# SyncE issues attention's loads and stores in the order of the program's steps

## The chip, the cores and the metric

The kernel runs on one core of one Trainium2 chip. The metric is the device time of one execution in microseconds (us). A core has five engines with an instruction queue each: TensorE (PE, matmuls), VectorE (DVE), ScalarE (ACT), GpSimd (POOL) and SyncE (SP). SP computes nothing here: it starts DMAs and reads a few numbers into its registers. Every queue runs in its own order, and an instruction that waits for a semaphore holds everything behind it in the same queue.

## The reference

Attention with a feature map comes first, then a mixture of experts. `phi` projects 64 values of a head to 128, subtracts the largest magnitude, and takes the exponentials of both signs.

```python
def phi(x):
    proj = np.einsum('bhsd,df->bhsf', x, w_phi)
    proj = proj - np.max(np.abs(proj), axis=-1, keepdims=True)
    return np.concatenate([np.exp(proj), np.exp(-proj)], axis=-1)
q_p, k_p = (phi(q), phi(k))
kv = np.einsum('bhsf,bhsd->bhfd', k_p, v)
z = np.sum(k_p, axis=2)
num = np.einsum('bhsf,bhfd->bhsd', q_p, kv)
den = np.einsum('bhsf,bhf->bhs', q_p, z)[..., None] + 1e-06
attn = num / den                      # 8 batches, 8 heads, 576 tokens, 64
...
x = attn.transpose(0, 2, 1, 3).reshape(4608, 512)
do_compute = x @ w_skip > 0           # the other tokens pass through
logits = xc @ w_gate                  # 8 experts, the largest is taken
h = np.maximum(xc[mask] @ w1[e], 0.0) # 512 -> 1024
y[mask] = gate_w[mask, None] * (h @ w2[e])
out[do_compute] = xc + y
```

## The kernel before

Matmuls run in fp32, or in two parts: a number is split into `hi` (rounded) and `lo` (the rest), and products of the parts are added.

**Units and items.** Attention works in units: four heads of one batch, of k or of q. There are 16 k units and 16 q units. A unit has five items: item 0 is the tail of 64 tokens, items 1 to 4 are four groups of the rest. Item s of the k stream is item s % 5 of k unit s // 5, and the same for q.

**Steps.** One loop (L724) goes through steps t. A stage with a lag works at step t on item t - lag of the k stream and on item t - 6 - lag of the q stream (`CFG["off"]` is 6). The order of the stages within a step is E, P, A, Z, U, T:

- T, lag 0 (`f_t`, L712): VectorE transposes a piece of the unit's `raw` tile (L289, L291; items 0, 1 and 3 only), ACT makes `hi` (L292), POOL or VectorE makes `lo` (L294). At item 0 of unit u it also issues the load of unit u + 1 of its stream (`st_load`, L256, four DMAs). So k unit u + 1 is loaded at step 5u, and q unit u + 1 at step 5u + 6. Four `raw` tiles exist, two for each stream in effect.
- P, lag 1 (`st_proj`): TensorE projects (L306 to L308), VectorE takes the maximum and subtracts it (L312, L321). Three PSUM banks.
- E, lag 3: exponentials; for k, POOL adds them up (`z`), for q, TensorE transposes first (L366).
- U, lag 4: k items are multiplied with `v` (L388, tails L395); q items with the k unit's sums (L486, L465), then `norm` on VectorE (L437 to L449) writes `xm`, `lgm`.
- Z and A, lags 5 and 6: sums over tokens and the augmented k sums.

Then, each step, `st_loadv` loads v of the k unit whose item 0 is one step old (L265, four DMAs, two buffers) and `st_loadvt` its tails at three steps (L274, four DMAs, two tiles).

**Stores.** What has to come some steps later stands in a list `later`, which is worked off at the head of a step (L730). When q item 4 of a batch's first unit is done, half of its rows go to `xrows` two steps later (`store_half`, L503 and for every second batch L505). When its second unit is done, `post(b)` computes the gate: a chain of some 14 small VectorE and ACT instructions (L538 to L561). Two steps later the other half goes out together with the gate (`store_rows`, L564, L566). Four steps later comes the rank among tokens (`rank`), five later `index`, seven later the copy of the rows to `out` (`rest`, L630 in four DMAs, L635 in four for every second batch). Two buffers of `xm` exist. After batch 5, `pick` chooses two experts and gathers their first tokens early.

**Order.** The program is traced in the order above. A scheduler then orders each engine's instructions by when it expects them to be ready, and by their place in the program where several are. Two things bind it: dependencies between tiles, and a manual schedule, inside which the named engines keep the program's order. Before the change PE has such a guard, from step 8 to step 78 (L725 to L728). SP has none.

**After attention.** The experts take their tokens in slots; weights come in 96 chunks of 512 KB through four `raw` buffers (L184, L187), are split by ACT (L188) and POOL or VectorE (L189), and multiplied (L881 to L913). Before the first chunk SP reads the chosen expert's number into a register (L1056).

Of the kernel before, what the change touches and what calls it, by code (L numbers as in the profile page):

```python
# [18 lines left out]
P = 128  # L19
# [5 lines left out]
def kernel(  # L25
# [25 lines left out]
    NAUG = D + E + 2  # L51
    NA1 = NAUG - 1
    # a row of xrows: the token, its gate, its number
    XW = DM + 2
    EB = B - 3
    NTE = 9 * (EB // 2) + 9
    # slots: full ones, ones of up to 192 tokens, ones of up to 128
    NSD = (NTOK + E * 63) // SLOT
# [22 lines left out]
    nc.scalar.activation(out=warm, in_=warm, func=AF.Exp)  # L81
    # w_phi in the rows of either head of a pair, and which rows are whose
    wsrc = const.tile([P, NF], F32, name="wsrc")
# [22 lines left out]
    iota_p = const.tile([P, P], F32, name="iota_p")  # L106
    # the tails of a quad's v, each pair in its own rows, zeros in the other's
    vts = [const.tile([P, 2, 2, D], F32, name="vt%d" % j) for j in range(2)]
# [14 lines left out]
    pad0 = const.tile([P, 2, 2], I32, name="pad0")  # L123
    # of every slot: the rows to gather and the rows to scatter to
    ft = const.tile([P, NSL, 4], I32, name="ft")
# [84 lines left out]
    def places(g, pad, v):  # L210
        # v is 0 in an empty place, else 1 + the row to gather; what to add so that no row is scattered from an empty one
        nc.vector.tensor_scalar(out=g, in0=v, scalar1=-1.0, scalar2=0.0, op0=ALU.add, op1=ALU.max)
        nc.vector.tensor_scalar(out=pad, in0=v, scalar1=0.0, scalar2=BIG, op0=ALU.is_equal, op1=ALU.mult)

    early = []
    # ------------------------------------------------------------------ attention
    with ExitStack() as actx:
# [4 lines left out]

        # a head is 32 runs of 18 tokens; partition (half of d, head of the pair, run)
        kv_in = {
# [4 lines left out]
        outv = out.rearrange("(b p j) m -> b p j m", p=32, j=18)  # L229
        # rows of xrows: two batches after each other, then the tails of both  # L230
        xr = xrows.rearrange("(b x) m -> b x m", x=2 * S)
# [201 lines left out]
        def norm(o, xdst, ldst, shape):  # L433
            # o: [P, 4, NAUG]
            den = small.tile([P, 4], F32, tag="den", name="den")
            rec = small.tile([P, 4], F32, tag="rec", name="rec")
            nc.vector.tensor_scalar(  # L437
                out=den.rearrange("p (t o) -> p t o", o=1), in0=o[:, :, NA1:NAUG],
                scalar1=1e-6, scalar2=None, op0=ALU.add,
            )  # L440
            nc.vector.reciprocal(out=rec, in_=den)
            rv = rec.rearrange("p (t o) -> p t o", o=1)
            a, c = shape

            def sh(x):
                return x.rearrange("p (a c) d -> p a c d", a=a)

            nc.vector.tensor_tensor(out=xdst, in0=sh(o[:, :, 0:D]), in1=sh(rv.broadcast_to([P, 4, D])), op=ALU.mult)
            nc.vector.tensor_tensor(  # L449
                out=ldst, in0=sh(o[:, :, D:NA1]), in1=sh(rv.broadcast_to([P, 4, NA1 - D])), op=ALU.mult)  # L450

        def st_use_q(u, i):
# [5 lines left out]
            if i == 0:  # L458
                # the tails of two batches side by side
                for h in range(4):  # L460
                    pr, hd = h // 2, h % 2
                    for half in range(2):
                        for par in range(2):
                            g = u.g - NQ * (1 - par)
                            nc.tensor.matmul(  # L465
                                ov[par * 64:par * 64 + 64, h, :],
                                et_of[g][:, half, hd * P + pr * 64:hd * P + pr * 64 + 64], kva_of[g][:, half, h, :],
                                start=(half == 0), stop=(half == 1),
                            )
                if u.hq == 0:  # L470
                    xt_of[u.b // 2] = (
                        xp.tile([P, 1, XW], F32, tag="xt", name="xt"),
                        xp.tile([P, 1, H, E + 1], F32, tag="lgt", name="lgt"),
                    )
                xt, lgt = xt_of[u.b // 2]
                norm(ov, xt[:, :, u.hq * 4 * D:(u.hq + 1) * 4 * D].rearrange("p a (h d) -> p a h d", d=D),
                     lgt[:, :, u.hq * 4:(u.hq + 1) * 4, :], (1, 4))
                return
# [34 lines left out]
        def post(b):  # L513
# [40 lines left out]
            )  # L554
            # the gate goes with the token's row
            nc.vector.tensor_reduce(out=ss[:, 0:nt], in_=ex[:, 0:nt], axis=AX.X, op=ALU.add)
# [20 lines left out]
            def rank():  # L577
                # rank of each computed token among those of its expert
                r = bank("O")[:, 0:nt * E]
# [66 lines left out]
        def pick(j):  # L646
            # the expert with the most tokens so far: its first tokens make a slot of their own, done early;
            # the ranks of its later tokens start anew
            cn = bank("O")[:, 0:E]
# [72 lines left out]

        man = None
        for t in range(n + OFF + LA):  # L724
            if CFG["man"] and t == CFG["man"][0]:  # L725
# [27 lines left out]
            if t == 1:  # L753
                setup()

    # ------------------------------------------------------------------ experts
    pools = {}
# [31 lines left out]
    def hidden_c(hv):  # L789
        # 192 tokens: the last 64 with both their parts next to each other  # L790
        hh = mo.tile([P, 2, SLOT], F32R, tag="hh", name="hh", bufs=5)
        hlo = mo.tile([P, 2, SLOT], F32R, tag="hlo", name="hlo", bufs=5)
        n = P + 64
        nc.scalar.activation(out=hh[:, :, 0:n], in_=hv[:, :, 0:n], func=AF.Relu)
        for o, a, b in ((hlo[:, :, 0:P], 0, P), (hh[:, :, n:SLOT], P, n)):
            (nc.gpsimd if (CFG["cp"] >> (a == P)) & 1 else nc.vector).scalar_tensor_tensor(  # L796
                out=o, in0=hv[:, :, a:b], scalar=0.0, in1=hh[:, :, a:b].bitcast(F32), op0=ALU.max, op1=ALU.subtract)
        return hh.rearrange("p f t -> p (f t)"), hlo.rearrange("p f t -> p (f t)")

    def half1(ws, xs):  # L800
        # a slot of 128 tokens: the tokens' columns stay, the weights stream
        _, xh, xl, _, _ = xs
# [38 lines left out]
    def store_c(y, xs):  # L841
        xg, to = xs[0], xs[3]
        # the sums of the high and of the low parts of 64 tokens lie in either half of y
        g, x, r = xg[1][:, DM:DM + 1], xg[1][:, 0:DM], slice(0, 64)
# [10 lines left out]
    def mm1(ws, xs, hooks=()):  # L855
# [3 lines left out]
        for c, (wh, wl) in enumerate(ws):  # L859
            if n < SLOT:  # L860
                # fewer than 256 columns take as long as 256: the products with both parts of x side by side
                hsum = mo.tile([P, 2, n], F32, tag="hsum", name="hsum")
# [65 lines left out]

    # the slots of the tokens that are left: per expert full ones of 256, a rest of up to 192 or of up to 128 in
    # one of its own kind  # L930
    eid = const.tile([1, NSL], I32, name="eid")
# [4 lines left out]
    def tables():  # L936
# [23 lines left out]
        nc.vector.tensor_tensor(out=exc, in0=inc, in1=nn, op=ALU.subtract)  # L960
        # a token's column: its rank, in groups of 128, plus cf[0] where it is below cf[1], else plus cf[2]
        nc.vector.tensor_scalar(out=cf[:, 0], in0=exc[:, 0], scalar1=2.0, scalar2=1.0, op0=ALU.mult, op1=ALU.add)
# [6 lines left out]
        nc.vector.tensor_tensor(out=cf[:, 2], in0=cf[:, 2], in1=cf[:, 1], op=ALU.subtract)  # L969
        # the experts of the slots, and how many there are  # L970
        le = const.tile([1, NSL, E], F32, name="le")
# [6 lines left out]
        nc.vector.tensor_scalar(out=eid[:, 0:NSL], in0=ef, scalar1=float(E - 1), scalar2=None, op0=ALU.min)  # L978
        # the column of each token
        rk = const.tile([P, NT], F32, name="rk")  # L980
# [44 lines left out]
        places(ft[:, NS2:NSL, 0:1], ft[:, NS2:NSL, 2:3], ix[:, 2 * NS2:NCOL].rearrange("p (t s) -> p t s", s=1))  # L1025
        # the slots that the sequence below leaves
        ov = const.tile([1, 8], F32, name="ov")
# [6 lines left out]
        for c, to, left in ((0, 0, "DC"), (1, 3, "CS")):  # L1034
# [9 lines left out]
            out=ovf[:, 0:NSL], in0=lv[:, 1], scalar1=float(num["D"] - 1), scalar2=float(NSL - 1), op0=ALU.add, op1=ALU.min)  # L1044
    # the slots in their order; a half one goes along with a full one
    phases = []
# [48 lines left out]

    # whatever the slots above don't hold
    nx = nc.values_load(ovf[0:1, NSL:NSL + 1], min_val=0, max_val=NSL)  # L1097
# [37 lines left out]
```

## Time and profile before

| | us |
|---|---|
| median of 3 runs | 684.47 |
| lowest and highest run | 684.28, 689.55 |
| span of the profiled execution | 681.4 |
| first expert matmul (L881) begins | 389.78 |

The page gives busy time by engine, a strip of 40 slices with busy tenths, and groups of instructions. An answer of the trace in order of time has start, duration, engine, line and what the instruction writes and reads; in square brackets stands how long the engine was idle before it and what ended that. `SPq` is SP's queue, and the duration of one of its DMAs is the time for which SP was occupied by starting it, not the transfer. A view of waits has the waiting instruction, what it waited for, then the total, the number of times and the longest.

This is the strip of the page, and the largest waits of SP's queue in the whole span:

```profile
PE   4897999979998889999899991999999989979994
DVE  6868888887978978978998799679988876677830
DMA  9898664857675667655316387269788877774500
```

```profile
SPq L184 <- POOL w L189: 53.7, 15, 14.8
SPq L187 <- POOL w L189: 48.6, 20, 6.2
SPq L256 <- DVE m L312: 47.0, 18, 5.7
...
SPq L503 <- DVE lgm L449: 15.1, 2, 9.3
SPq L630 <- DVE lgm L449: 14.0, 3, 6.0
```

One slice is 17 us. Attention fills the first 22 or so, the experts the rest. The raw loads (L256) wait for VectorE, which frees their buffers; the name of the releaser is that of the instruction that ended last before the wait was over.

### The profile page before, as it was taken

To read this page: it belongs to the slowest core of one execution; us is meant where nothing else is said; L and a number is where in the kernel's file an instruction comes from. 1 tells how busy PE (TensorE), PEld (TensorE's weight loads), DVE (VectorE), ACT (ScalarE), POOL (GpSimd) and SP (SyncE) were. 2 spreads that over 40 slices of the span, in tenths; PEclk is the share of its full clock that TensorE was granted. 3 is DMA by queue.
4 is the path that set the end of the run, shared out by engine and by line. 5 is a ranking of instruction groups with operands and counts; after the bars stand their busy time and mean duration, and the time that the engine had idled before them with its cause. 6 is when DMAs were issued, how large, how long until landed. Compare 5 with 4: busy or idle time off the path is not lost. (4 is left out here: it accounts for less than half of the span.)

```text
span 681.4 us, 16258 instructions
## 1 busy us (share of the span) xinstructions
PE 600.5 (88%) x6045; PEld 514.2 (75%) x6045; DVE 539.6 (79%) x1216; ACT 373.7 (55%) x747; POOL 440.7 (65%) x383
## 2 busy tenths in 40 slices
PE   4897999979998889999899991999999989979994
PEld 3585888768877778877788881888878879868893
DVE  6868888887978978978998799679988876677830
ACT  4566665647565475656564533147757556555510
POOL 6886777777777596868774458276575485374411
PEclk9898999999999999999999996899989999999998
DMA  9898664857675667655316387269788877774500
GB/s 130 127 145 157 112 168 91 160 108 133 144 144 90 146 117 133 142 103 114 105 33 195 114 222 232 72 203 296 249 262 268 268 238 267 251 238 139 192 17 27
DMA packets 221684, 108.17 MB, mean 159 GB/s; under 512 B 160293, under 2 KB 202405, under 8 KB 221604
## 3 DMA queue, kind: packets, MB, share of 16 engines
q1 hardware_dynamic: 218272, 97.60, 58.8%
q0 software_dynamic: 3200, 9.45, 4.0%
q8 instruction: 49, 0.80, 0.5%
q14 instruction: 31, 0.25, 0.1%
q10 hardware_dynamic: 132, 0.07, 0.0%
HBM read 83.86 MB, written 24.02 MB: 158 GB/s over the span
## 5 line engine op out<-in xcount | busy, mean ns | idle before, releaser
L189 POOL TENSOR_TENSOR w<-wraw_c,w 128x1024 fp32r<-128x1024 f32 x45 | 109.9, 2454 | 70.6 <-ACT w L188 64.3
L188 ACT ACTIVATE w<-wraw_c 128x1024 fp32r<-128x1024 f32 x96 | 101.0, 1057 | 56.9 <-DMA wraw_c<-in_moe_w_dram 44.9
L353 POOL TENSOR_TENSOR z<-ek 128x512 f32<-128x512 f32 x64 | 81.7, 1277 | 54.9 <-ACT ek L345 45.1
L312 DVE TENSOR_REDUCE m<-ps_P 128x4 f32<-128x512 f32 (+1 forms) x160 | 96.4, 620 | 3.7 <-PE ps_P L308 3.6
L321 DVE TENSOR_TENSOR u<-ps_P,m 128x512 f32<-128x512 f32 (+1 forms) x160 | 95.9, 621 | 0.4
L306 PE MATMUL ps_P<-wph,hi 128*128 128x256 f32 x256 | 80.8, 316 | 16.6 <-ACT hi L292 8.5
L486 PEld LDWEIGHTS ps_O<-kva,eq 128*64 128x64 f32 x2048 | 75.2, 137 | 18.0 <-ACT eqt L373 7.3
L189 DVE TENSOR_TENSOR w<-wraw_c,w 128x1024 fp32r<-128x1024 f32 x51 | 75.4, 1481 | 14.6 <-ACT w L188 14.5
L486 PE MATMUL ps_O<-kva,eq 128*64 128x74 f32 x2048 | 78.4, 229 | 5.0 <-ACT eqt L373 3.2
L294 POOL TENSOR_TENSOR lo<-xT,hi 128x512 fp32r<-128x512 f32 x61 | 78.1, 1280 | 5.0 <-ACT hi L292 4.8
L308 PE MATMUL ps_P<-wph,lo 128*128 128x256 f32 x256 | 73.4, 287 | 0.0
L307 PE MATMUL ps_P<-wpl,hi 128*128 128x256 f32 x256 | 73.2, 286 | 0.0
L388 PE MATMUL ps_K<-ek,v 128*64 128x256 f32 x512 | 71.3, 396 | 1.5 <-DMA v<-in_v_dram 1.5
L372 ACT ACTIVATE eq<-ps_U 128x512 f32<-128x512 f32 x64 | 37.9, 593 | 57.2 <-PE ps_U L366 49.2
L306 PEld LDWEIGHTS ps_P<-wph,hi 128*128 128x128 f32 x256 | 49.4, 193 | 20.4 <-ACT hi L292 9.0
L908 PE MATMUL ps_O<-w,hh 128*128 128x512 f32 x160 | 62.4, 400 | 1.4 <-DVE hh L796 1.3
L836 POOL DMA_INDIRECT out_dram<-o,si x17 | 22.2, 1305 | 54.1 <-DVE o L834 44.4
L913 PE MATMUL ps_O<-w,hlo 128*128 128x512 f32 x120 | 49.0, 410 | 5.1 <-DVE hlo L796 5.1
L307 PEld LDWEIGHTS ps_P<-wpl,hi 128*128 128x128 f32 x256 | 49.7, 194 | 0.0
L308 PEld LDWEIGHTS ps_P<-wph,lo 128*128 128x128 f32 x256 | 49.6, 194 | 0.2 <-DVE lo L294 0.2
L366 PE MATMUL ps_U<-ident,u 128*128 128x128 f32 x288 | 48.4, 286 | 0.6 <-DVE u L321 0.6
L289 DVE STREAM_TRANSPOSE xTt<-raw 128x128 f32<-128x128 f32 x32 | 9.9, 309 | 48.8 <-DMA raw<-in_k_dram 26.8
(233 smaller groups left out, 1570.9 us busy)
## 6 DMA issues: line engine op xcount, KB each, us to landing
wraw_c<-in_moe_w_dram SPq DMA_DIRECT2D x96, 512.0 KB, 4.6
raw<-in_k_dram SPq DMA_DIRECT2D x64, 144.0 KB, 4.0
raw<-in_q_dram SPq DMA_DIRECT2D x64, 144.0 KB, 4.1
v<-in_v_dram SPq DMA_DIRECT2D x64, 128.0 KB, 3.7
out_dram<-xm SPq DMA_DIRECT2D x32, 256.0 KB, 4.4
xrows<-xm SPq DMA_DIRECT2D x8, 516.0 KB, 4.2
xrows<-xm SPq DMA_DIRECT2D x8, 512.0 KB, 4.7
vt<-in_v_dram SPq DMA_DIRECT2D x64, 16.0 KB, 2.6
```

The lines of the kernel that those rows point to most:

```text
L188: nc.scalar.activation(out=hi, in_=raw, func=AF.Copy)
L189: (eng or nc.vector).tensor_tensor(out=lo, in0=raw, in1=hi.bitcast(F32), op=ALU.subtract)
L294: (nc.vector if CFG["ini"][nlo[0] - 1:nlo[0]] == "v" else nc.gpsimd).tensor_tensor(out=lo, in0=xT, in1=hi.bitcast(F32), op=ALU.subtract)
L306: nc.tensor.matmul(o, hi[:, c], wph, start=True, stop=False)
L307: nc.tensor.matmul(o, hi[:, c], wpl, start=False, stop=False)
L308: nc.tensor.matmul(o, lo[:, c], wph, start=False, stop=True)
L312: nc.vector.tensor_reduce(out=m[:, 0:nt], in_=pv, axis=AX.X, op=ALU.max, apply_absolute_value=True)
L321: nc.vector.tensor_tensor(out=uu[:, 0:nt, :], in0=pv, in1=m[:, 0:nt].rearrange("p (t o) -> p t o", o=1).broadcast_to([P, nt, NF]), op=ALU. ...
L353: zeng.tensor_tensor(out=z, in0=e[:, 0:2, :], in1=e[:, 2:4, :], op=ALU.add)
L388: nc.tensor.matmul(o[hd * 64:hd * 64 + 64, :], u.v[:, 2 * pr + hd, g * D:(g + 1) * D], u.e[i][:, 2 * j + hd, :], start=(g == 0), stop=False,)
L486: nc.tensor.matmul(ov[s * 64:s * 64 + 64, 2 * j + hd, :], e[:, half, j, hd, s * 64:s * 64 + 64], kva[:, half, 2 * pr + hd, :], start=(half ...
L908: nc.tensor.matmul(y[sub], hh[:, t], wh[:, fi, :], start=first, stop=False)
```

## The change

The loop over the steps is put into a second manual schedule, for SP, from the first step to the last. Inside it SP issues its DMAs in the program's order: at each step first what `later` holds, then the raw loads, then v, then the tails. The first k unit's load (called at L698, before the loop), the last batch's copy to `out` and all that belongs to the experts stay outside. Nothing is fenced at the guard's end by the code. Some comment lines go, so the lines after shift little.

```diff
         man = None
+
+        sman = actx.enter_context(ExitStack())
+        sman.enter_context(tc.manual_schedule(engines={mybir.EngineType.SP}))
         for t in range(n + OFF + LA):
             if CFG["man"] and t == CFG["man"][0]:
                 man = ExitStack()
                 man.enter_context(tc.manual_schedule(engines={mybir.EngineType.PE}))
             if CFG["man"] and t == CFG["man"][1]:
                 man.close()
...
             if t == 1:
                 setup()
+        sman.close()
```

## Prediction

> **What bounds the kernel now.** I read the page for the whole, busy time by stretch for the stage that the change touches, then the waits of PE and DVE in it, and last SP's queue and DVE in order of time. Times are us from the span's start; in a timeline the columns are start, duration, engine, line, what it does.
>
> ```profile
> span 681.4 us, 16258 instructions
> PE 600.5 (88%) x6045; PEld 514.2 (75%) x6045; DVE 539.6 (79%) x1216; ACT 373.7 (55%) x747; POOL 440.7 (65%) x383
> ```
> ```profile
> core 0: us, PE busy (x) PEld busy (x) DVE busy (x) ACT busy (x) POOL busy (x), PEclk, DMA share, GB/s
> 60.00:345.00 285.00, 263.35 (x3470) 221.72 (x3469) 240.46 (x680) 175.12 (x415) 216.06 (x206) 1.00 0.61 125
> ```
> ```profile
> DVE xTt L289 <- DMA raw<-in_k_dram: 20.6, 11, 2.4
> DVE xTt L289 <- DMA raw<-in_q_dram: 16.5, 10, 3.4
> ...
> PE ps_O L619 <- POOL rhs L608: 7.5, 6, 1.6
> PE ps_P L306 <- DVE u L321: 5.9, 9, 1.5
> PE ps_O L486 <- ACT eqt L373: 3.2, 4, 1.1
> PE ps_O L486 <- DVE lgm L449: 1.4, 2, 0.8
> PE ps_O L406 <- DVE acc L625: 1.3, 3, 0.7
> PE ps_P L306 <- DVE km L549: 1.1, 1, 1.1
> PE ps_O L580 <- DVE lgm L449: 1.1, 1, 1.1
> ```
>
> The second fence is the steady part of attention: PE is busy 263.35 of 285 at full clock (92%), in an order fixed by its own guard. The third holds the waits of DVE and PE there. DVE is busy 240.46 and idle 44.5, of which 20.6 + 16.5 = 37.1 is spent in front of a transpose whose raw tile has not landed; 7.4 is left. PE waits for DVE in all 5.9 + 1.4 + 1.3 + 1.1 + 1.1 = 10.8, and for no DMA in this stretch. So PE sets the pace, DVE is close behind, and a late raw load reaches PE only by way of DVE.
>
> **How far SP's order differs from the program's.**
>
> ```profile
> 93.54 3.31 SPq L256 DMA_DIRECT2D raw<-in_k_dram  x4
> ...
> 103.87 2.19 SPq L256 DMA_DIRECT2D raw<-in_q_dram  x3
> 106.15 0.82 SPq L503 DMA_DIRECT2D xrows<-xm  x1
> 107.02 0.64 SPq L256 DMA_DIRECT2D raw<-in_q_dram  x1
> ...
> 120.37 2.08 SPq L265 DMA_DIRECT2D v<-in_v_dram  x4
> 122.55 0.84 SPq L274 DMA_DIRECT2D vt<-in_v_dram  x2
> ...
> 129.77 3.51 SPq L630 DMA_DIRECT2D out_dram<-xm  x4
> ...
> 139.34 0.57 SPq L564 DMA_DIRECT2D xrows<-xm  x1
> 140.01 0.57 SPq L566 DMA_DIRECT2D xrows<-xt  x1
> ```
> ```profile
> 90.09 0.57 SPq L564 DMA_DIRECT2D xrows<-xm  x1
> ...
> 323.61 0.57 SPq L564 DMA_DIRECT2D xrows<-xm  x1
> ```
> ```profile
> 112.19 0.31 DVE L289 STREAM_TRANSPOSE xTt<-raw 128x128 f32<-128x128 f32 x1 [2.92 <-DMA raw<-in_q_dram]
> ...
> 128.29 0.18 DVE L449 TENSOR_TENSOR lgm<-ps_O,rec 128x36 f32<-128x36 f32 x1
> ...
> 139.20 0.12 DVE L561 RECIPROCAL xt<-gt 128x1 f32<-128x1 f32 x1
> ```
>
> Batch b's gate store L564 belongs to the step at which post(b) has run plus 2: post(1) runs at step 29 (item 19 of the q stream, plus off 6, plus lag 4), its store at the head of step 31. Loads of q unit u stand at step 5(u-1)+6, so q unit 6 (the seventh q load, 103.87) stands at step 31 too, behind the store. In the trace it goes out 35 ahead of it. The next four v loads of step 31 go at 120.37, 19 ahead of the store. After the change both stand behind L564, and L564 waits for the gate chain on DVE, whose last piece ends at 139.32. From one even batch's store to another odd one's, 90.09 to 323.61, lie five batches of ten steps: 233.52 / 50 = 4.67 per step.
>
> **The change part by part.** It adds no arithmetic and removes none; 318 DMAs of attention on SP (252 of raw, v and vt loads, 2 of gate weights, 24 stores to xrows, 40 to out) keep their size and number, and those after the first 50 us change their place.
>
> *Stores moved up.* L503, L505, L564, L566, L630 and L635 no longer follow later steps' loads. Nobody in attention reads xrows or out before the early gather, so an earlier store gains nothing. Cost 0; that holds as long as the tile of two batches on (two buffers) is not waiting for it.
>
> *Loads moved down, behind the gate store.* Queued behind the waiting L564 are q unit 6 (4 DMAs), v of k unit 6 (4), its tails (4), k unit 8 (4), then the next stores and q unit 7. With L564 at 139.34 as now, SP issues L564 and L566 (1.24 to 140.6), four q loads (2.19 + 0.64, to 143.4) and four v (2.08, to 145.5).
>
> ```profile
> raw<-in_q_dram SPq DMA_DIRECT2D x64, 144.0 KB, 4.1
> v<-in_v_dram SPq DMA_DIRECT2D x64, 128.0 KB, 3.7
> ```
>
> With these medians from issue to landing the q tile lands at 147.5 and v at 149.2. PE did step 29 up to DVE's norm at 128.47. It first needs v of k unit 6 at step 35 (item 31 plus lag 4): 128.47 + 6 x 4.67 = 156.5, a cover of 7.3. It needs q unit 6 at step 37: 165.8, a cover of 18.3, of which a transpose and the split into hi and lo take an estimated 4. K unit 8 follows after vt (four at 0.42) and four issues of 0.83: issued by 150.5, wanted at step 41, 184.5. So the loads that are 35 later still arrive in time for PE, once per batch, with v the closest. Cost on PE's path 0; what hides it is PE's own work of steps 30 to 34, and if the gate chain ended 8 later, each further us would be paid seven times.
>
> *DVE's waits for raw tiles.* The scheduler places a transpose where it expects the tile, and DVE then stands. Now that is 37.1 over some 10.5 pairs of units, 3.5 a pair. What it becomes behind long runs of DMAs is not in the steady part; the nearest rows are the start, where SP's order is already that of the steps, with 16 DMAs between one k unit and the next:
>
> ```profile
> 31.85 3.26 SPq L256 DMA_DIRECT2D raw<-in_k_dram  x4
> ...
> 43.75 4.24 SPq L256 DMA_DIRECT2D raw<-in_k_dram  x4
> ```
> ```profile
> 38.66 0.31 DVE L289 STREAM_TRANSPOSE xTt<-raw 128x128 f32<-128x128 f32 x1 [1.56 <-DMA raw<-in_k_dram]
> ...
> 43.06 0.31 DVE L289 STREAM_TRANSPOSE xTt<-raw 128x128 f32<-128x128 f32 x1 [1.06 <-DMA raw<-in_q_dram]
> ...
> 51.23 0.31 DVE L289 STREAM_TRANSPOSE xTt<-raw 128x128 f32<-128x128 f32 x1 [3.97 <-DMA raw<-in_k_dram]
> ...
> 55.21 0.31 DVE L289 STREAM_TRANSPOSE xTt<-raw 128x128 f32<-128x128 f32 x1 [0.61 <-DMA raw<-in_q_dram]
> ```
>
> Those two pairs stand 1.56 + 1.06 = 2.6 and 3.97 + 0.61 = 4.6. The lower end for the steady part is 0 a pair (no tile late any more), which would give DVE 37.1 back and PE at most its 10.8 of waits. Between two gate stores, ten steps, stand 16 raw, 8 v and 8 vt loads and on average 9 stores, 41 DMAs. The upper end takes the worse pair for every 16 of them: 4.6 x 41 / 16 = 11.8 per batch in place of 7.0, or 28 over six batches. I take 4.6 a pair, because the runs get longer, not shorter: 1.1 x 10.5 = 11.6 more on DVE, of which PE feels the share that it feels now, 10.8 / 37.1 = 0.29: +3.4.
>
> SP's issue time carries this term: in the rows above four raw loads take 2.8 to 4.2 of SP and land 4.1 after. The Trainium skill says of this (DMA: Bandwidth & Descriptors, section "Issuing engines are not separate DMA queues") that the time in which a sequencer starts a DMA is usually small beside the DMA; by that the run's length would not matter and the sum would be 0. These rows contradict it here, so I keep +3.4.
>
> *The end of attention.*
>
> ```profile
> 362.68 3.23 SPq L630 DMA_DIRECT2D out_dram<-xm  x4
> 366.12 0.92 SPq L184 DMA_DIRECT2D wraw_c<-in_moe_w_dram  x1
> 368.01 0.53 SPq L564 DMA_DIRECT2D xrows<-xm  x1
> ```
> ```profile
> 384.38 1.05 ACT L188 ACTIVATE w<-wraw_c 128x1024 fp32r<-128x1024 f32 x1
> ```
>
> The weights' first loads lie outside the guard and can go before or after these stores. They are out from 366.12 and ACT splits the first chunk only at 384.38, so ten us either way are covered: 0. If they had to wait for the last gate store they would start some 31 later; nothing in the code ties them to it.
>
> Sum: 0 + 0 + 3.4 + 0. The profiled span is 681.4, the median of the runs 684.47, 3.07 more, which I keep: 684.47 + 3.4 = 687.9.
>
> **The rivals.** *DVE becomes the bound (slower).* At the upper end DVE stands 28 longer. It has 7.4 of other idle time to give; what is beyond that is paid in full: +20.6, 705. For it: busy 240.46 plus 37.1 of standing is 97% of the stretch. Against: two pairs at the start show no growth from one to the next run beyond 2.
>
> *Late v starves PE (slower).* Decides once L564 goes out more than 7.3 later against PE than now. At 12 later each of seven batches pays 5: +35, 719. Against: the gate chain's instructions are small and earlier in the program than what delays them. The Trainium skill's advice to issue a DMA early and wait late (DMA: Bandwidth & Descriptors, "Rules for kernel authors") points to this rival; no row of this case shows PE short of v in the stretch.
>
> *DVE stops standing (faster).* Loads no longer follow directly on the transpose that frees their buffer, and the tile could be there before DVE gets to it. That takes the 37.1 away and with it up to 10.8 of PE: 673.7. It decides when the load leads DVE's place for it by more than the 4.1 of landing. Against: DVE's order is made for the earliest place, so it moves with the load.
>
> **How the numbers follow.** Likeliest, the covers hold and DVE stands a little longer: 0.53, 687.9, own range 681 to 692. DVE bound: 0.22, 692 to 706. Late v: 0.08. No standing: 0.17, 673 to 681. A range of 676 to 706 leaves out late v and about half of the last. One per cent is 6.8, about what a measurement of this kernel tells from no change: below 677.6 lie 0.13 (most of no standing); above 691.3 lie 0.22 + 0.08 and 0.03 of the likeliest, 0.33; between them 0.54.
>
> **What would show it.** Right: in SP's queue the q load stands behind L564 in its step, waits of SP sit at L564 and L503, PE in the steady stretch still waits for no v, and DVE's waits for raw lie between 37 and 49. Wrong: PE waiting for v or vt at L388 or L395; DVE's waits for raw over 60 or under 20; weights that start only after the last L564.

## The result, and the profile after

| us | before | after |
|---|---|---|
| median of the runs | 684.38 (682.85 to 689.55, 4 runs) | 736.99 (733.11 to 738.56, 4 runs) |
| ratio to before | | 1.073, 95% interval 1.068 to 1.079 |
| span of the profiled execution | 681.4 | 731.3 |
| first expert matmul begins (L881, after L885) | 389.8 | 439.6 |

The change costs 52.6 us. The forecast, 687.9 in a range of 676 to 706, was wrong by 49. Lines behind L754 lie four higher after the change.

All of it is lost ahead of the experts: they take 270.4 us from their first to their last such matmul before (389.8 to 660.2), and 270.6 after (439.6 to 710.2).

The strip of the page after, 18.3 us a slice:

```profile
PE   3889889759879859879859999289997989998994
...
PEclk9999999989999979999989999689999999998998
DMA  8876186095287087186075277627888788685500
GB/s 129 128 106 117 41 157 135 2 184 125 41 168 136 1 170 155 39 155 134 7 170 109 89 209 211 204 92 218 264 256 276 256 246 285 230 262 176 192 16 25
```

Up to us 340 the DMA row before never fell under 3. Now there are slices with 2, 1 and 7 GB/s (the 8th, 14th and 20th): for nearly 20 us at a time next to nothing is loaded. In the slice after each of them PE falls to 5 tenths and PEclk to 8 or 7.

To compare the same work I take the stretch from the first to the last matmul L619 over the ranks. First before, then after: the row of that line (instructions, then shortest, median and longest in ns, then first and last start), and busy time in that stretch, in the columns of the prediction's second fence:

```profile
L619 PE MATMUL ps_O<-rhs,OP x54: 175/176/178, 99.1 to 331.9; 128*128 128x32 bf16 x54
```
```profile
99.10:331.90 232.80, 212.94 (x2820) 179.10 (x2820) 195.37 (x554) 139.76 (x332) 175.30 (x168) 1.00 0.62 127
```
```profile
L619 PE MATMUL ps_O<-rhs,OP x54: 176/186/189, 103.6 to 378.5; 128*128 128x32 bf16 x54
```
```profile
103.60:378.50 274.90, 222.43 (x2823) 184.01 (x2822) 197.75 (x557) 142.43 (x333) 177.90 (x170) 0.95 0.55 109
```

The stretch takes 42.1 longer; 4.5 more are lost ahead of it and 3.3 behind it, 49.9 in all. For the same matmuls (2820 and 2823) PE is busy 9.5 longer, at a granted clock of 0.95 in place of 1.00, and stands 52.5 in place of 19.9: 32.6 more. So some three quarters of the loss are standing and one quarter is a slower clock.

SP's waits of the same stretch, before and after (instruction, what it waited for, total, times, longest):

```profile
SPq L256 <- DVE m L312: 37.2, 12, 5.7
SPq L256 <- DVE u L321: 18.5, 5, 4.5
...
SPq L564 <- DVE xt L561: 10.6, 3, 4.2
```
```profile
SPq L564 <- DVE xt L561: 62.6, 3, 20.9
SPq L564 <- DVE xm L561: 31.1, 2, 15.7
SPq L503 <- DVE lgm L449: 18.0, 5, 4.6
```

Before, SP stood mostly at raw loads for a free buffer: it was as far ahead as four buffers allow. After, it waits for a buffer only 2.2 in all (v and vt). It stands at stores, 18.7 a time at L564 (93.7 in 5), with the loads behind them. One such place in full, in order of time: SP's queue, then DVE, then POOL, then PE.

```profile
121.32 3.54 SPq L256 DMA_DIRECT2D raw<-in_k_dram  x4
145.85 0.56 SPq L564 DMA_DIRECT2D xrows<-xm  x1
...
147.57 3.91 SPq L256 DMA_DIRECT2D raw<-in_q_dram  x4
```
```profile
145.70 0.13 DVE L561 RECIPROCAL xt<-gt 128x1 f32<-128x1 f32 x1
...
148.94 0.20 DVE L591 TENSOR_REDUCE rki<-rm 128x5 int32<-128x40 f32 x1
...
152.91 0.71 DVE L291 STREAM_TRANSPOSE xT<-raw 128x512 f32<-128x512 f32 x1 [3.34 <-DMA raw<-in_q_dram]
153.54 0.13 DVE L592 TENSOR_SCALAR rkp<-rki 128x5 int32<-128x5 int32 x1
```
```profile
153.84 2.95 POOL L594 TENSOR_SCALAR OP<-iota_p,rkp 128x128 bf16<-128x128 f32 x5 [5.68 <-DVE RKH L596]
156.77 1.27 POOL L353 TENSOR_TENSOR z<-ek 128x512 f32<-128x512 f32 x1
157.99 1.26 POOL L294 TENSOR_TENSOR lo<-xT,hi 128x512 fp32r<-128x512 f32 x1
159.21 0.72 POOL L608 TENSOR_TENSOR rhs<-rm,ids 128x320 bf16<-128x320 bf16 x1
```
```profile
159.99 0.42 PE L619 MATMUL ps_O<-rhs,OP 128*128 128x32 bf16 x10 [7.41 <-POOL rhs L608]
```

From 124.86 to 145.85 SP starts nothing. L564 is released at the end of the gate chain (145.83), the q load behind it goes out from 147.57, and DVE stands 3.34 at its transpose. Behind that transpose in DVE's order stands rkp, whose input was ready at 149.14. POOL then does z and lo ahead of rhs, 2.45 more, and PE, whose order is fixed, stands 7.41 at L619. The same place before the change, where POOL goes from OP straight to rhs:

```profile
147.26 0.40 PE L619 MATMUL ps_O<-rhs,OP 128*128 128x32 bf16 x10 [1.61 <-POOL rhs L608]
```

The stand is 5.80 longer, as much as DVE's 3.34 and POOL's 2.45 together. Three of the six batches look so (stands of 7.41, 7.79 and 7.39). In the other three DVE stands as long at the same transpose, 3.23 to 3.63, but ahead of the whole rank chain, and L619 stands as before. Here is one, DVE and then PE:

```profile
205.34 0.71 DVE L291 STREAM_TRANSPOSE xT<-raw 128x512 f32<-128x512 f32 x1 [3.32 <-DMA raw<-in_q_dram]
```
```profile
213.64 0.35 PE L619 MATMUL ps_O<-rhs,OP 128*128 128x32 bf16 x8 [0.88 <-POOL rhs L608]
```

From the L619 of one batch to that of the next it nevertheless takes 7.4 to 9.4 longer every time, so this stand is one place of several. Over the stretch PE stands 25.2 in front of L619 (7.5 before) and 14.8 at L306 for DVE's u (5.3 before). The next gate store needs a gate chain, and that needs PE and DVE to go on, so the loss adds up from batch to batch: L564 leaves 6.5 later than before at the place above, and 40.5 later four batches on (364.10 after, 323.61 before).

The clock is read from stretches of 4 us around that stand, and from 3 us behind a shorter one; the third value from the end is PEclk:

```profile
148.00:152.00 4.00, 4.00 (x54) 3.42 (x54) 1.57 (x9) 2.12 (x4) 0.16 (x1) 1.00 0.86 174
...
156.00:160.00 4.00, 0.01 (x1) 0.01 (x1) 2.94 (x9) 1.46 (x3) 4.00 (x6) 0.57 0.84 131
160.00:164.00 4.00, 4.00 (x34) 3.36 (x33) 2.02 (x5) 0.85 (x3) 2.90 (x4) 0.57 1.02 240
164.00:168.00 4.00, 4.00 (x57) 3.58 (x53) 1.11 (x3) 1.85 (x6) 2.68 (x3) 1.00 0.46 125
170.00:173.00 3.00, 3.00 (x15) 1.51 (x15) 1.98 (x4) 0.52 (x3) 1.72 (x2) 0.54 0.70 196
```

After the stand PE runs at 0.57 for some 4 us: 34 matmuls in a full stretch where 54 and 57 fit at 1.00. The Trainium skill (TensorE: Matmul & The Clock Gate, section "Part 1: The HAM clock gate (the "warmup" mystery)") says that the array's clock is halved after an idle window of some 3.4 us and comes back after a busy window as long. The trace agrees for this stand: the longest in the stretch before was 1.6, and the clock there was 1.00 throughout. Shorter stands than that window lowered it too: 1.67 ahead of the matmul at 169.74 (0.54 in the last row) and 2.00 ahead of 241.51 (0.50 from 242 to 244). Others of 1.79 to 2.35 in the same stretch left it at 1.00, so what decides there is open.

### The profile page after: what moved, and what is told of

It is laid out like the page before. It is cut to its first block, busy times and chain, and to the rows that moved or that the text cites. A ratio compares the mean times of both kernels' runs of the same rounds, so it can differ in the third digit from the quotient of the medians.

```text
span 731.3 us, 16198 instructions
## 1 busy us (share of the span) xinstructions
PE 611.8 (84%) x6045; PEld 520.0 (71%) x6045; DVE 538.9 (74%) x1216; ACT 375.2 (51%) x747; POOL 442.5 (60%) x383
## 5 line engine op out<-in xcount | busy, mean ns | idle before, releaser
L306 PE MATMUL ps_P<-wph,hi 128*128 128x256 f32 x256 | 83.0, 324 | 30.9 <-DVE u L321 21.6
L189 DVE TENSOR_TENSOR w<-wraw_c,w 128x1024 fp32r<-128x1024 f32 x51 | 76.5, 1504 | 14.8 <-ACT w L188 14.8
L291 DVE STREAM_TRANSPOSE xT<-raw 128x512 f32<-128x512 f32 x64 | 44.9, 703 | 44.5 <-DMA raw<-in_q_dram 30.2
L306 PEld LDWEIGHTS ps_P<-wph,hi 128*128 128x128 f32 x256 | 51.3, 200 | 36.6 <-issue 19.1
L308 PE MATMUL ps_P<-wph,lo 128*128 128x256 f32 x256 | 75.2, 294 | 0.0
L307 PE MATMUL ps_P<-wpl,hi 128*128 128x256 f32 x256 | 74.9, 293 | 0.0
L307 PEld LDWEIGHTS ps_P<-wpl,hi 128*128 128x128 f32 x256 | 51.6, 202 | 0.0
L308 PEld LDWEIGHTS ps_P<-wph,lo 128*128 128x128 f32 x256 | 51.4, 201 | 0.2 <-DVE lo L294 0.2
```

Of the source, the lines that this page charges most:

```text
L189: (eng or nc.vector).tensor_tensor(out=lo, in0=raw, in1=hi.bitcast(F32), op=ALU.subtract)
L306: nc.tensor.matmul(o, hi[:, c], wph, start=True, stop=False)
L307: nc.tensor.matmul(o, hi[:, c], wpl, start=False, stop=False)
L308: nc.tensor.matmul(o, lo[:, c], wph, start=False, stop=True)
```

## The experiments

Theory A: loads stand behind stores that wait, and DVE then stands at the raw tiles. Theory B: the loads come late because each is issued in its own step. Theory C: the long stores L630 and L635 in front of loads cost the time. Except where it says otherwise each starts from the changed kernel. The kernel before was timed beside each of them and took 681.9 to 683.3; the 737.0 of the changed kernel stand beside 684.4, so differences to it are good to some 3. Beside the gate stores alone, the half's stores alone, the third buffers alone and the third buffers with the short stores on ScalarE the kernel before spread from 675.5 to 688.9, and these four intervals are wide.

| | us | ratio to before, 95% interval |
|---|---|---|
| changed kernel | 737.0 | 1.068 to 1.079 |
| short stores (L503, L505, L564, L566) on ScalarE | 700.4 | 1.026 to 1.035 |
| gate stores alone on ScalarE | 711.2 | 1.036 to 1.054 |
| half's stores alone on ScalarE | 751.3 | 1.092 to 1.115 |
| short stores one step later | 743.8 | 1.086 to 1.103 |
| gate stores three steps later | 714.6 | 1.047 to 1.057 |
| short stores three steps later | 724.2 | 1.059 to 1.069 |
| third v and vt buffer | 732.2 | 1.060 to 1.084 |
| loads first in each step | 716.7 | 1.045 to 1.058 |
| loads first, third v and vt | 718.8 | 1.048 to 1.058 |
| short stores on ScalarE, third v and vt | 702.7 | 1.023 to 1.042 |
| short stores on ScalarE, loads first | 692.5 | 1.010 to 1.024 |
| the same, fifth raw buffer | 695.4 | 1.013 to 1.025 |
| short stores on ScalarE, loads first, third v and vt | 683.4 | 0.999 to 1.005 |
| rank matmul two steps later | 726.0 | 1.059 to 1.069 |
| before: short stores on ScalarE | 680.4 | 0.995 to 1.002 |
| before: fifth raw buffer | 682.6 | 0.998 to 1.004 |
| before: rank matmul two steps later | 685.7 | 1.001 to 1.007 |

### Which stores hold the loads

ScalarE issues the short stores; its order stays the scheduler's. There are 24 of them; the 36 of the expectations is a miscount.

```diff
-                        nc.sync.dma_start(out=rowm[b][:, :, c], in_=xm[:, :, c])
+                        nc.scalar.dma_start(out=rowm[b][:, :, c], in_=xm[:, :, c])
```

> The four short stores of each batch (L503, L505, L564, L566) leave SyncE and are issued by ScalarE, whose order stays the scheduler's; SyncE's loads and the long stores L630 and L635 stay in the order of the steps. Theory A (the loads stand behind stores that wait for the gate chain and the norm): SyncE's 158.4 us of waits at L564 and L503 go and the loads run ahead to the limit of their buffers again; 684 to 697, of which up to 8 for the issue of 36 stores on ScalarE. Theory B (the loads are late because each is issued in its own step, whatever stands between them): 725 to 740, as the changed kernel. Theory C (most of the loss is the rows of the long stores L630 and L635 moved in front of loads): 720 to 740.

> Only the gate stores L564 and L566 are issued by ScalarE; L503 and L505 stay on SyncE in the order of the steps. Theory A with the gate store as the main blocker: 703 to 713, the half's store keeping some 40 to 50 us of SyncE's waits. If either blocker alone is enough: 725 to 738.

> Only L503 and L505 are issued by ScalarE; the gate stores stay on SyncE in the order of the steps. Theory A with the gate store as the main blocker: 722 to 735. If L503 counts as much as the gate store: 710 to 720.

All four: 700.4, a gain of 37 out of 53, between A's range and the others. Only the gate stores: 711.2, as A has it, 26 of the 37. But SP's waits did not fall as expected: it now stands at L503, for 107.3 from 60 to 370, where 40 to 50 were expected and 18.0 had been. So the sum of SP's waits doesn't price the loss.

```profile
SPq L503 <- DVE lgm L449: 107.3, 6, 19.5
```

B and C, which expected 720 and more of the run with all four, can't be the whole of it. Only the half's stores: 751.3, 14 slower, expected by no theory. There SP is done with the loads at 113.86 and stands until the gate store, 35.4 us:

```profile
110.76 3.10 SPq L256 DMA_DIRECT2D raw<-in_k_dram  x4
149.32 0.56 SPq L564 DMA_DIRECT2D xrows<-xm  x1
```

So with one of two blocking stores gone, SP comes to the other sooner and waits there longer. Why the whole is slower than with both was not settled.

With all four gone SP's largest wait, from 60 to 370, is a load's:

```profile
SPq L265 <- PE ps_K L388: 111.0, 12, 12.9
```

That is v, waiting for one of its two buffers, with vt and the next k load behind.

### Stores moved to later steps

```diff
-                later.append((now[0] + 2, store_rows))
+                later.append((now[0] + 5, store_rows))
```

The runs below have 3 or 5 in that place, for one or both of the short stores.

> Only the gate stores L564 and L566 move, three steps later than in the changed kernel (five after their batch instead of two), behind q, v and vt; the store of the first half, L503, stays in front of its q load. Theory A with the gate store as the main cause (119.9 of SyncE's 158.4 us stood there): 700 to 712, with L503 left as the rest. Theory A with any of the two stores enough to hold the loads: 718 to 730. Theory B and C: 728 to 740.

> L503, L505, L564 and L566 all move three steps later than in the changed kernel, right in front of the next k load. Theory A: SyncE seldom waits at them and the time is 684 to 697. Theory B and C: 725 to 740.

> L503, L505, L564 and L566 are placed one step later than in the changed kernel (three steps after their batch instead of two), so the q load and the v load that stood right behind each of them stand right in front of it; vt and the next k load still stand behind it. Theory A, if the q and v loads are what counts: 690 to 705. Theory A, if the next k load behind the same store counts as much: 705 to 722. Theory B and C: 728 to 740.

The gate stores alone: 714.6, slightly over A's range. Both stores by three steps: 724.2; both by one: 743.8. These two miss A's ranges; 724.2 lies just under the range of B and C for that run, and 743.8 above theirs, so they don't speak for A by themselves. The trace shows a second effect. L503 now waits longer at SP, 111.6 from 60 to 370 where both moved by three steps, and DVE's norm waits for the stores of `xm` (9.7 in all, 6 times):

```profile
SPq L503 <- DVE lgm L449: 111.6, 6, 22.3
```

In the built program L503 then waits for the last norm that was written ahead of it into the tile `xm`, which is one of a later step and writes other columns (moved by three steps it leaves at 128.37 behind the norm at 128.26, the last but one of the second unit; in the changed kernel it left before any of that unit's norms into `xm`). A store that stands later in the program thus waited for more, not for less.

### Loads first in each step

The stores of a batch fall due at steps 26, 31 and 36 (for batch 1), and each of these steps also issues a q load and a v load, behind them. Here each step issues its loads first; the stores keep their step.

```diff
             now[0] = t
+            for items, us, off in streams:
+                x = t - off
+                if x == CFG["ql"]:
+                    st_load(us[0])
+                if 0 <= x < n and items[x][1] == 0 and x // 5 + 1 < len(us):
+                    st_load(us[x // 5 + 1])
+            run_stage(LU - 3, lambda u, i: st_loadv(u) if (i == 0 and u.kind == "k") else None)
             for w, f in [x for x in later if x[0] <= t]:
```

> All three stores of a batch fall due at the start of a step that also issues a q load and a v load, and stand in front of both. Here each step issues its k, q and v loads first and then its stores; SyncE stays in the order of the steps, and all stores stay on it. The order on SyncE is that of the run with the stores one step later (743.8), but L503 waits for its own norm alone, not for one a step later. Theory A in the form that it is the q load right behind a store on which VectorE then stands: 690 to 712. Theory A, if the next k load behind the store holds VectorE as well: 712 to 732. If the later norm was not what made the one-step run slow: 740 to 747.

> The short stores are issued by ScalarE, and each step issues its loads ahead of the long stores L630 and L635, which stay on SyncE. If what was left of the loss with the short stores on ScalarE (700.4) is the q load behind L630: 684 to 694. If it is ScalarE's issuing, or the order of the loads among themselves: 698 to 704.

> Loads first in each step and the third buffers, with all stores on SyncE in the order of the steps. With loads first alone (716.7) SyncE stood 87.0 us at L564 and 28.7 us at the v load, and VectorE stood 35.2 us at k tails. If the gate store in front of the next k load is the rest: 710 to 718, the third buffers bring little. If v's buffer is: 690 to 700.

Loads first alone: 716.7, 20 less, in the range for the next k load behind the same store holding DVE as well. Against the one-step run it is 27 faster; the order on SP differs only in the long stores, which stand behind q and v here, so the later norm and the long stores share these 27. SP's and DVE's waits from 60 to 370 in it:

```profile
SPq L564 <- DVE xt L561: 49.8, 3, 16.7
SPq L564 <- DVE xm L561: 37.2, 3, 14.3
```
```profile
DVE xTt L289 <- DMA raw<-in_k_dram: 35.2, 11, 5.8
DVE xTt L289 <- DMA raw<-in_q_dram: 14.6, 10, 4.3
```

DVE's largest wait has moved from q to the tail of k, the load that is still behind L564. Third buffers for v do not help there (718.8, just over the range that expected so): the store holds the k load, not v. With the short stores on ScalarE, loads first brings 700.4 to 692.5. The long stores in front of q and v were thus worth some 8: C has a share, but a small one. What is left on SP's queue is v's wait in front of the k load: 115.5 in 12, the longest 14.4.

### The last waiting DMA

```diff
-    vts = [const.tile([P, 2, 2, D], F32, name="vt%d" % j) for j in range(2)]
+    vts = [const.tile([P, 2, 2, D], F32, name="vt%d" % j) for j in range(3)]
...
-            u.v = ld.tile([P, 4, 4 * D], F32, tag="v", name="v")
-            u.vt = vts[u.g % 2]
+            u.v = ld.tile([P, 4, 4 * D], F32, tag="v", name="v", bufs=3)
+            u.vt = vts[u.g % 3]
```

> The changed kernel with a third buffer for v and a third vt tile, all stores where the change puts them. Theory A: the loads are held by the stores and not by buffers (SyncE waits 4 us in all for v and vt there), so 730 to 740. If buffers are the cause: 690 to 715.

> As the run with the short stores on ScalarE, with a third buffer for v and a third vt tile. With those stores gone SyncE stood 111.0 us (12 times, longest 12.9) at the v load for its buffer, with vt and the next k load behind it. If this wait is what is left of the loss (v's program place in front of the next k load): 682 to 691. If what is left is ScalarE's issuing of 36 stores, or the long stores in front of loads: 697 to 703, as without the third buffers.

> Short stores on ScalarE, each step's loads ahead of its long stores, and a third buffer for v and a third vt tile. Without the third buffers (692.5) SyncE stood 115.5 us (12 times) at the v load for its buffer with vt and the next k load behind, and VectorE stood 26.3 us at k tails. If each DMA that waits in front of a load is one part of the loss, this takes the last one: 681 to 688. If a rest is due to the order of the loads itself or to ScalarE's issuing: 690 to 696.

Alone the third buffers leave the changed kernel as it was (732.2), and with the short stores on ScalarE too (702.7): there SP then stood at the long stores, with q behind them:

```profile
SPq L630 <- DVE lgm L449: 55.7, 6, 15.2
```

With the short stores on ScalarE and the loads first, they are worth 9: 683.4, ratio 1.002 to before. So issuing each load in its own step costs nothing that can be measured once no DMA that waits stands in front of it, which takes B away. The stretch between the L619s, DVE's waits for raw in it, and SP's largest:

```profile
101.10:332.80 231.70, 213.39 (x2821) 179.06 (x2821) 194.40 (x554) 140.47 (x332) 175.38 (x168) 1.00 0.61 125
```
```profile
DVE xTt L289 <- DMA raw<-in_q_dram: 15.8, 8, 3.2
DVE xTt L289 <- DMA raw<-in_k_dram: 15.3, 9, 2.2
```
```profile
SPq L256 <- DVE xT L291: 54.8, 9, 7.1
```

231.7 against 232.8 before, at clock 1.00. SP stands at raw loads for a free buffer again, as it did before the change, and not at stores. DVE still stands 31.1 at raw tiles, about the 32.9 of the kernel before; what that standing costs, the two equal times don't tell.

> The kernel before, in the scheduler's order, with the same short stores issued by ScalarE; no part of the change. It prices ScalarE's issuing of 36 stores by itself. If that costs nothing or frees the loads a little: 677 to 685. If it is what was left in the run with loads first (692.5): 688 to 695.

The control without the change: 680.4, so issuing 24 stores on ScalarE costs nothing that can be measured, and it isn't the reason for the gains above.

### More raw buffers

A fifth raw buffer, in the kernel with loads first and short stores on ScalarE, and in the kernel before.

```diff
-            u.raw = ld.tile([P, 2, 18, 32], F32, tag="raw", name="raw", bufs=4)
+            u.raw = ld.tile([P, 2, 18, 32], F32, tag="raw", name="raw", bufs=5)
```

> As the run before it, with a fifth raw buffer. If the loads could run further ahead and the stand at the raw tiles is what remains: 676 to 690, and 6 or more below the run before it. If buffers don't bind in the order of the steps: the same as that run within 4.

> The kernel before, in the scheduler's order, with a fifth raw buffer; no part of the change. SyncE waited there 64 us for a raw buffer to come free, and VectorE 37 us for raw tiles. If VectorE's wait for raw tiles reaches the end of attention at a fair share: 668 to 678. If it lies beside TensorE's work: 680 to 685.

695.4 and 682.6: no gain in either. In the kernel before DVE still stands 34.9 at raw tiles (18.5 for q, 16.4 for k, from 60 to 370), so the run does not price that standing; it shows that a buffer more doesn't remove it. No version beat the kernel before by more than its runs vary.

### Where DVE's stand reaches PE

```diff
-CFG = {..., 'post': (4, 5, 7), ...}
+CFG = {..., 'post': (4, 7, 7), ...}
```

> The changed kernel with one number changed: the matmul over the ranks (L619) stands in TensorE's order seven steps after its batch instead of five. In the changed kernel TensorE stood 25.2 us in front of it, for the rank chain that VectorE had behind a raw transpose. If this matmul is where VectorE's stands reach TensorE, most of the 17.7 us that it stands longer than before goes, and some of the clock's 9.5: 710 to 722. If TensorE then stands at the next thing that VectorE owes it: 728 to 740.

> The kernel before with the same number changed, as the control; TensorE stood 7.5 us there in front of L619. 674 to 680 if those 7.5 are on the path, 681 to 685 if they move on to the next wait.

726.0, 11 less, between the two ranges; the control is 2.4 over before. PE's wait for POOL's rhs at L619 is gone from the largest ones, and its wait for DVE's u has grown, over the whole span from 22.3 (18 times) to

```profile
PE ps_P L306 <- DVE u L321: 34.2, 19, 4.0
```

So the matmul over the ranks is one door through which DVE's stand reaches PE, for some 11 to 13 of the 53. Closed, the stand comes in at the next one.

## Why the prediction was wrong

**What bounds.** That PE sets the pace and a late raw load reaches it only by way of DVE was right: after the change PE's large waits in the stretch are for DVE and POOL, and none is for v.

**SP's order.** Right: the q load stands behind L564, and SP's waits sit at L564 and L503.

**Stores moved up, cost 0.** Nearly right of the stores themselves: ACT's gate write waits 12.8 in all for `out` stores of the tile's last use, where the condition named a buffer not yet free; it was not priced alone. What stands behind the stores belongs to the next step.

**Loads moved down, cost 0.** This is the step that failed. Its covers, 7.3 for v and 18.3 for q, were measured to the step at which PE first needs the tile, with L564 leaving at the time of before. But the first to need the q tile is DVE's transpose. It stands in DVE's order right where the load lands, in three of the six batches with rkp of the same batch's rank chain behind it, and PE needs that chain (L619, step 34) three steps ahead of the q tile (step 37). The cover to that place was none: DVE stood 3.34, and 3.2 to 3.7 in each batch. L564 itself left only a little later against PE: 42.3 behind the L619 of the batch before, where it had been 40.2, and 1.3 to 3.5 later at the other places, well inside the 7.3. So the time of the store was nearly right, and the place to which the cover was measured was wrong. In place of 0, the loads behind the gate stores cost some 26: taking these stores alone off the queue gave that back.

**DVE's waits for raw tiles, +3.4.** The size was too small and the share wrong. In the same work they grew from 32.9 to 55.7, 22.8 where 11.6 was taken; the upper end of 28 was close. The share of 0.29 was that of the old places, which had slack. In the new places PE stood 32.6 more, over the whole of it. The sum of these waits says little without the place: with the short stores on ScalarE DVE stood 28.5 at raw tiles from 60 to 370, 23.7 for q and 4.8 for k, less than the 37.1 of the kernel before, and the run still lost 18.

In the same stretch of time as the prediction's third fence they came to 57.2: past the 49 that it named, short of its 60. What mattered on the queue was not SP's issue time, by which this term was argued, but a wait in it; and one load of the prediction's rows held SP for 0.7 to 1.1 against 4.1 to landing, so those rows did not contradict that starting a DMA is the smaller part. The Trainium skill (DMA: Bandwidth & Descriptors, section "Rules for kernel authors") says of spreading DMAs over the issuing engines that it only saves issue time. For loads behind a store that waits the runs differ: the short stores on another queue gave 37.

**The end of attention, 0.** Of the right kind: from the last L619 to the end 3.3 are lost, all of them ahead of the first expert matmul. These were not taken apart.

**The clock.** No term of the sum had it. In the stretch it is 9.5: matmuls at half clock follow the stands of 7.41 and 7.79 and those of 1.67 and 2.00. With the short stores on ScalarE PE stood only 4.2 longer than before, yet was busy 8.1 longer. It has five stands of 3.05 to 4.04 in its stretch, and the clock is 0.50 behind each; one is the 3.19 ahead of 250.43 (another of 1.84 ends 4.4 ahead of it). Its stretch between the L619s, and 4 us behind that stand:

```profile
104.40:349.50 245.10, 221.03 (x2825) 185.16 (x2823) 196.47 (x551) 143.55 (x333) 176.09 (x168) 0.95 0.59 121
```
```profile
252.00:256.00 4.00, 4.00 (x36) 2.97 (x36) 2.73 (x5) 1.07 (x3) 3.62 (x4) 0.50 0.22 29
```

**The rivals.** "DVE becomes the bound" had the right side and the right place of standing, but by its rule (what is over 7.4 of idle time is paid) 22.8 gives 15.4, 700. It holds for total busy time and not for a chain that passes DVE, POOL and PE once a batch. "Late v" did not happen. Its turning point, L564 going out more than 7.3 later against PE, was for the wrong load.

**What stays open.** How much is data that came late and how much is the scheduler's new plan: DVE, ACT and POOL were ordered anew in each kernel, and no run held their orders fixed. At L619 the plan's part can be read: POOL's z and lo ahead of rhs take 2.4 at each of the three long stands, 7.3 of the 17.7 that PE stands longer there; that rkp lies behind the transpose is the plan's doing too. Also why taking only the half's stores off is slower.

## What to carry to other kernels

Before a queue's order is fixed, list each DMA in it that waits for a computed result, and what stands behind it; give it another queue or put the loads in front, or else the prefetch ends there, however many buffers there are. Measure a late load's cover to the first engine that touches the tile, in that engine's order, with what stands behind it, and not to the engine that sets the pace. Several such waits in a row hide one another: here three had to go (stores, long stores, v's buffer) until the time of before was back, and the third alone was worth nothing.

## What the runs showed of the hardware

A stand in PE's order costs more than itself. In the changed kernel and in the run with the short stores on ScalarE, all nine stands of 3.05 us and more between us 95 and 380 were followed by matmuls at a granted clock of 0.50; the 4 us after the one of 7.41 had a mean clock of 0.57, with 34 matmuls where 57 fit next. Stands of 3 us are no threshold: of six between 1.67 and 2.35 in the changed kernel two did the same, the one of 1.67 among them, and four did not. The 1.6 of the kernel before left the clock at 1.00.
